# Block means of v copied by VectorE, identity matmuls ahead of the scores, masking in one operation and moved steps in an attention + two-MLP kernel

## The chip, the cores and the metric

The kernel runs on one core of one Trainium2 chip. The metric is the device time of one execution in microseconds; the median of three runs is given, and one execution was profiled. Engines are named as the profile names them: PE (TensorE, matmuls; PEld its weight loads), DVE (VectorE), ACT (ScalarE), POOL (GpSimd), SP (SyncE, which here issues most DMAs).

## The reference

The input is a batch of 2, with 8 heads, 768 positions and a head size of 64. Each query attends to its neighbours at a distance under 16 and, besides, to one summary for each block of 32 positions: the maximum of the block's keys, and the mean of its values.

```python
k_sum = k.reshape(B, H, nb, block, D).max(axis=3)
v_sum = v.reshape(B, H, nb, block, D).mean(axis=3)
scores_l = scale * np.matmul(q, k.transpose(0, 1, 3, 2))
mask_l = np.abs(pos[:, None] - pos[None, :]) < window
scores_s = scale * np.einsum('bhsd,bhnd->bhsn', q, k_sum) + np.log(block)
scores_all = np.concatenate([np.where(mask_l, scores_l, -1e9), scores_s], axis=-1)
a = np.exp(scores_all - np.max(scores_all, axis=-1, keepdims=True))
a = a / (np.sum(a, axis=-1, keepdims=True) + 1e-09)
attn = np.matmul(a, np.concatenate([v, v_sum], axis=2))
...
x = attn as 1536 tokens of 512
x = (silu(x @ w_gate) * (x @ w_val)) @ w_out      # 512 -> 1536 -> 512
out = relu(x @ w_in) ** 2 @ w_out2                # 512 -> 2048 -> 512
```

The weights arrive as 64-bit floats (read as pairs of 32-bit words), so that they have to be converted on the chip.

## The kernel before

**Tiling.** The 1536 tokens are three sets of 512. A set has four pairs of heads, and a pair has two units of 4 blocks of 64 queries. One unit is a tile of 128 rows (2 heads x 64 queries) by 480 columns: for each of the 4 blocks 96 neighbouring keys (64 and a halo of 16 on either side) and 24 summaries. Keys come in tiles `kw`, queries in `q`, values in `v`: 96 rows of values and under them, in rows 96 to 119, the 24 block means of v.

**Steps of a unit.** `sum_k` takes the blocks' maxima (DVE) and `fill_k` copies them into `kw` (POOL or DVE). `scores` or `masked_scores` multiplies (PE, into a PSUM bank). In the first set the mask is added by PE (`ident` times `mask`), and `tops` takes row maxima (DVE); in the other sets `masked` scales, masks and takes minima on DVE, four operations of 120 columns each with a read of the accumulator. Exponentials follow on ACT (`masked_exps`, `exps`), then `recip`, a normalisation (`norm` on POOL or `norm_act` on ACT), `turn` (transposes on PE), `turned` (a copy by ACT), `product` with v (PE), and `high` and `low`, which split the result into a float32r part and a rest.

**Means of v.** `load_vn` loads a tile of 4 heads' v, `sum_v` adds it up on POOL in three steps, `mean_v` multiplies by `sel` on PE, `keep_v` copies the result into `vs`, and `load_vs` spreads it by DMA into rows 96 to 119 of the `v` tiles: from ACT's queue in the prologue (eight DMAs), from SP's later.

**Weights.** A chunk of weights is converted in five pieces: `magnitude` (ACT), then clamp, shift, sign, low (DVE). `split_chunk` then makes `whi` (ACT) and `wlo` (DVE). Every product is three matmuls (xh whi, xl whi, xh wlo). Converted chunks are stored to DRAM (`keep_chunk`) and loaded again for the later sets (`load_kept`).

**Order.** It is written by hand; nothing reorders it. The prologue is the attention of set 0: a loop over t = 0 to 11 runs one step of several units in each turn. Then come 36 periods "12" (12 chunks of the first MLP for each of three sets) and 48 periods "34" (16 for each set). A period has three slots: the multiplications of w_gate (j = 0), those of w_val (j = 1), and the second product of the period before. The attention of sets 1 and 2 is placed into these slots by `place`: `first`, `after` and `late` are lists of steps for each slot, a pair of heads takes 6 slots (two periods), and `s` is its slot of scores. `pieces_of` puts the pieces of the weights into the slots.

**Pools.** There are two PSUM banks for the attention of the sets 1 and 2 (`ps_a`), two for the first products (`ps_m`) and four for the second (`ps_c`). The tile `raw` has three buffers, `wf` three, `v` three, `q` two, `kw` three, `vn` two. A DMA issue waits, besides the buffer, for the landing of the DMA that stood eight issues before it.

## Time and profile before

| | us |
|---|---|
| median of 3 runs (662.18 to 662.78) | 662.76 |
| the profiled execution | 661.7 |
| its span | 660.0 |
| PE busy | 627.9 (95%) |
| DVE busy | 417.9 (63%) |
| ACT busy | 340.0 (52%) |
| POOL busy | 40.1 (6%) |

The shares are means over the whole span. The prologue ends near 57 us, set 0 of the first MLP near 180 us, the periods "12" near 391 us. A matmul's end is modelled, so that a busy PE can still run below its peak; a gap before one is real. In a row of the timeline the bracket gives the idle time before the instruction and what ended it. The granted clock is TensorE's, 1.00 for 2.4 GHz and 0.50 for 1.2 GHz.

### The profile page before, as it was taken

The page shows a single profiled execution, that of the slowest core. Times are in us where ns is not written, and L with a number is a line of the kernel's source. Part 1 is how long each engine was busy: PE and PEld are TensorE (multiplying, and loading weights), DVE is VectorE, ACT ScalarE, POOL GpSimd, SP SyncE. Part 2 cuts the span into 40 slices and gives each one's busy share as a digit, 9 for nine tenths or more (in the row PEclk, how much of TensorE's full clock was granted, in tenths as well). Part 3 has the DMA queues.
Part 4 walks back from the last instruction along what each step waited for, and adds up shares of the span by engine and source line. Part 5 has one row for each costly group of instructions (what it writes and reads, how often), then busy time and mean ns, then how long its engine had stood idle before and what let it go on. Part 6 is the DMA issues. An engine that isn't in the chain of part 4 may idle for free.

```text
span 660.0 us, 8823 instructions
## 1 busy us (share of the span) xinstructions
PE 627.9 (95%) x3208; PEld 517.1 (78%) x3208; DVE 417.9 (63%) x622; ACT 340.0 (52%) x606; POOL 40.1 (6%) x54
## 2 busy tenths in 40 slices
PE   5768889999999999999999999999999999999997
PEld 4756678777888888788888888888888888888885
DVE  3667998998675777678776656444455444544443
ACT  1555388668457677845434435444444444444442
POOL 4423500000000000000000000000000000000000
PEclk9889999999999999999999999999999999999999
DMA  8989999862976885656858233222143222342211
GB/s 338 325 290 354 299 329 319 279 209 94 345 265 229 273 278 205 197 181 217 294 189 288 98 121 128 96 100 97 66 160 128 96 95 96 107 149 96 95 49 64
DMA packets 52908, 126.02 MB, mean 191 GB/s; under 512 B 9856, under 2 KB 16000, under 8 KB 51328
## 3 DMA queue, kind: packets, MB, share of 16 engines
q1 hardware_dynamic: 51232, 125.06, 55.7%
q10 hardware_dynamic: 1632, 0.39, 0.4%
q8 instruction: 25, 0.41, 0.3%
q14 instruction: 19, 0.16, 0.1%
HBM read 103.28 MB, written 20.97 MB: 188 GB/s over the span
## 4 chain that ended last, share of the span: by engine, by line
PE 78%; DVE 9%; ACT 5%; DMA 5%; issue 2%; POOL 1%; SPq 0%; DVEq 0%; ACTq 0%; POOLq 0%
PE bank L501 22%; PE bank L510 20%; PE bank L529 19%; PE bank L527 11%; DMA kept<-wf 2%; DVE wlo L211 2%; PE bank L445 1%; DVE wf L179 1%; DMA v<-vs 1%; ACT s L403 1%; DVE wf L174 1%; ACT wf L160 1%; PE bank L348 1%; DVE wf L163 1%; PE bank L433 1%
## 5 line engine op out<-in xcount | busy, mean ns | idle before, releaser
L211 DVE TENSOR_TENSOR wlo<-wf,whi 128x1024 fp32r<-128x1024 f32 (+2 forms) x85 | 123.5, 1454 | 52.5 <-ACT whi L210 51.6
L210 ACT CAST whi<-wf 128x1024 fp32r<-128x1024 f32 (+2 forms) x85 | 104.1, 1225 | 90.5 <-PE bank L529 50.0
L501 PE MATMUL bank<-xh,whi 128*128 128x512 f32 x288 | 116.5, 405 | 3.8 <-ACT g L729 1.9
L501 PE MATMUL bank<-xh,wlo 128*128 128x512 f32 x288 | 113.2, 393 | 4.5 <-DVE wlo L211 4.5
L501 PE MATMUL bank<-xl,whi 128*128 128x512 f32 x288 | 112.7, 391 | 0.0
L746 DVE TENSOR_TENSOR r<-r 128x512 f32<-128x512 f32 x48 | 33.2, 692 | 86.4 <-ACT hh L745 86.4
L529 PE MATMUL bank<-whi,hl 128*128 128x512 f32 x192 | 74.8, 390 | 0.0
L529 PE MATMUL bank<-whi,hh 128*128 128x512 f32 x192 | 74.7, 389 | 0.0
L529 PE MATMUL bank<-wlo,hh 128*128 128x512 f32 x192 | 74.7, 389 | 0.0
L510 PE MATMUL bank<-xh,whi 128*128 128x512 f32 x192 | 74.7, 389 | 0.0
L510 PE MATMUL bank<-xl,whi 128*128 128x512 f32 x192 | 74.7, 389 | 0.0
L510 PE MATMUL bank<-xh,wlo 128*128 128x512 f32 x192 | 74.7, 389 | 0.0
L744 ACT ACTIVATE r<-bank 128x512 f32<-128x512 f32 x48 | 28.7, 598 | 86.6 <-PE bank L510 86.6
L501 PEld LDWEIGHTS bank<-xh,wlo 128*128 128x128 f32 x288 | 54.2, 188 | 18.0 <-DVE wlo L211 6.6
L501 PEld LDWEIGHTS bank<-xh,whi 128*128 128x128 f32 x288 | 54.2, 188 | 16.5 <-ACT g L729 2.9
L734 ACT CAST hh<-g 128x512 fp32r<-128x512 f32 x36 | 22.2, 618 | 81.1 <-DVE g L733 81.1
L501 PEld LDWEIGHTS bank<-xl,whi 128*128 128x128 f32 x288 | 54.3, 189 | 10.1
L527 PE MATMUL bank<-hh,whi 128*128 128x512 f32 x144 | 57.5, 400 | 0.0
L527 PE MATMUL bank<-hl,whi 128*128 128x512 f32 x144 | 56.2, 390 | 0.0
L527 PE MATMUL bank<-hh,wlo 128*128 128x512 f32 x144 | 56.2, 390 | 0.0
L174 DVE SCALAR_TENSOR_TENSOR wf<-raw,wf 128x1024 uint32<-128x1024 uint32 (+2 forms) x29 | 41.9, 1446 | 0.3
L529 PEld LDWEIGHTS bank<-whi,hh 128*128 128x128 f32 x192 | 36.1, 188 | 7.6
(73 smaller groups left out, 907.0 us busy)
## 6 DMA issues: line engine op xcount, KB each, us to landing
wf<-kept SPq DMA_DIRECT2D x120, 256.0 KB
raw<-in_w_dram SPq DMA_DIRECT2D x44, 512.0 KB
kept<-wf SPq DMA_DIRECT2D x28, 512.0 KB
raw<-in_w_dram SPq DMA_DIRECT2D x12, 1024.0 KB
wf<-kept SPq DMA_DIRECT2D x24, 512.0 KB
kw<-in_kW_dram SPq DMA_DIRECT2D x8, 768.0 KB
q<-in_qB_dram SPq DMA_DIRECT2D x8, 512.0 KB
vn<-in_vN_dram SPq DMA_DIRECT2D x4, 768.0 KB
```

What stands on the lines that cost most here:

```text
L160: nc.scalar.activation(f32(w), f32(hw), ACTF.Abs)
L163: nc.vector.tensor_scalar(out=f32(w), in0=f32(w), scalar1=HI_MIN, scalar2=HI_MAX, op0=ALU.max, op1=ALU.min)
L174: nc.vector.scalar_tensor_tensor(out=w, in0=hw, scalar=0xC0000000, in1=w, op0=ALU.bitwise_and, op1=ALU.bitwise_or)
L210: lambda: nc.scalar.copy(hi[:, cs], t),
L211: lambda: nc.vector.tensor_sub(lo[:, cs], t, f32(hi[:, cs])),
L501: nc.tensor.matmul(p, w[a][:, c], x[i][kk], start=(kk == 0 and n == 0), stop=(kk == KD - 1 and n == 2),)
L510: nc.tensor.matmul(p, w[a][:, c], x[i][kk], start=(kk == 0 and n == 0), stop=(kk == KD - 1 and n == 2),)
L527: nc.tensor.matmul(ps[t], w[a][:, c], h[e], start=(f == 0 and n == 0), stop=(f == last and n == 2))
L529: nc.tensor.matmul(ps[t], h[e][:, t * P:(t + 1) * P], w[a][:, off:off + DM], start=(f == 0 and n == 0), stop=(f == last and n == 2),)
L734: nc.scalar.copy(h[0], g)
L744: nc.scalar.activation(r, p, ACTF.Relu)
L746: nc.vector.tensor_mul(r, r, r)
```

## The change

- `mean_v` writes its four heads at rows 0, 32, 64 and 96 (`sel` and `vs` have 128 rows), so that DVE can copy the means into rows 96 to 119 of `v`: in the prologue `put_vs` issues two copies for each pair of heads in place of DMAs on ACT's queue. In the later sets SP's DMAs stay. `mean_v` moves from turn 0 to turn 1, behind `recip` and `norm`.
- Eight matmuls of the identity with itself stand ahead of the first scores.
- `masked` becomes one scaled addition over 480 columns with `maskn` (made by POOL in turn 8) and one minimum.
- `product` of both units writes one bank; `high_both` and `low_both` take it in one operation each, one slot after the second product.
- In `place`, scores and masking move one slot earlier. In `pieces_of`, `keep_chunk` and `load_kept` move from slot 2 to slot 1, and `magnitude` to just behind the first copy of h.
- The first additions of the upper heads' `sum_v` move one turn earlier, the load of the first `v` behind the second pair's loads.

```diff
-    def sum_v(b, g, engine):
+    def sum_v(b, g, steps=(4, 2, 1)):
...
+        for n in steps:
+            nc.gpsimd.tensor_add(t[:, :, 0:n, :], t[:, :, 0:n, :], t[:, :, n:2 * n, :])
...
-                ps[0:4 * NS, 0:D], sel[:, i, :], t[:, i, 0, :], start=(i == 0), stop=(i == VG - 1)
+                ps[:, 0:D], sel[:, i, :, :], t[:, i, 0, :], start=(i == 0), stop=(i == VG - 1)
...
-        def load_vs(self, queue):
+        def put_vs(self, put):
...
-                    r = (h % 4) * NS
-                    queue.dma_start(
-                        out=self.v[WIN:W, at:at + n, j * D:(j + 1) * D],
-                        in_=vs[r:r + NS, b, h // 4, :].unsqueeze(1).to_broadcast([NS, n, D]),
+                    r = 32 * (h % 4)
+                    put(
+                        self.v[WIN:W, at:at + n, j * D:(j + 1) * D],
+                        vs[r:r + NS, b, h // 4, :].unsqueeze(1).to_broadcast([NS, n, D]),
...
-            for i in range(UB):
-                mv = self.variant(j, i)
-                c = slice(i * W, (i + 1) * W)
-                nc.vector.tensor_tensor_reduce(
-                    out=s[:, c], in0=ps[:, c], in1=mask[:, mv, :],
-                    scale=-SCALE, scalar=3.0e38, op0=ALU.add, op1=ALU.min,
-                    accum_out=m[:, i:i + 1],
-                )
+            nc.vector.scalar_tensor_tensor(
+                out=sv, in0=ps[:, 0:UB * W].rearrange("p (n c) -> p n c", c=W), scalar=-SCALE,
+                in1=maskn[:, mv:mv + UB, :], op0=ALU.mult, op1=ALU.add,
+            )
+            nc.vector.tensor_reduce(out=m, in_=sv, op=ALU.min, axis=AX.X)
...
+        def high_both(self, copy):
+            copy(self.x[0][self.hp], self.st["po", 0])
+
+        def low_both(self):
+            nc.vector.tensor_sub(self.x[1][self.hp], self.st.pop(("po", 0)), f32(self.x[0][self.hp]))
...
+        for hp, p in enumerate(pairs):
+            for j in range(2):
+                at(after, d0 + 6 * hp + 3 + j, lambda p=p, j=j: p.scores(j))
...
-                at(after, s + j, lambda p=p, j=j: p.scores(j))
-                at(first, s + j + 1, lambda p=p, j=j: p.masked(j))
+                at(first, s + j, lambda p=p, j=j: p.masked(j))
...
-                at(after, s + 10 + j, lambda p=p, j=j: p.product(j, ps_a))
-                at(first, s + 11 + j, lambda p=p, j=j: p.high(j, nc.vector.tensor_copy))
-                at(first, s + 11 + j, lambda p=p, j=j: p.low(j))
+                at(after, s + 10 + j, lambda p=p, j=j: p.product(j, ps_a, True))
+            at(first, s + 12, lambda p=p: p.high_both(nc.vector.tensor_copy))
+            at(first, s + 12, p.low_both)
...
+        busy = bank(ps_m)
+        for i in range(WARM):
+            nc.tensor.matmul(busy[:, 0:P], ident, ident, start=True, stop=True)
...
-            if t in (0, 5):
+            if t in (1, 5):
                 mean_v(0, t // 5, ps_m)
                 keep_v(0, t // 5)
-            go("recip", t - 1)
-            go("norm", t - 1)
+                pairs[t // 5 * 2].put_vs(nc.vector.tensor_copy)
+            elif t in (2, 6):
+                pairs[t // 6 * 2 + 1].put_vs(nc.vector.tensor_copy)
...
-            if t in (0, 5):
-                pairs[t // 5 * 2].load_vs(nc.scalar)
-                pairs[t // 5 * 2 + 1].load_vs(nc.scalar)
...
                     if s == 1:
                         load_words(k + 4)
-                    if s == 2:
                         keep_chunk(k + 1)
                         load_kept(k + 3)
-                        cv[k + 3] = convert_chunk(k + 3)
-                        cv[k + 3][0]()
...
                         nc.scalar.copy(h[0], g)
+                        magnitude()
                         c2[3]()
```

In the prologue, on DVE, from the maxima of the first pair's keys (`ks`, line 332, 334 in the changed kernel) on, it stands before:

```order
L332 TENSOR_REDUCE ks_192<-kw 128x24
L340 COPY kw<-ks_192 128x4x24 x2
L367 TENSOR_REDUCE m<-bank 128x4
L370 TENSOR_SCALAR m<-m 128x4
L276 COPY vs<-bank 96x64
L332 TENSOR_REDUCE ks_234<-kw 128x24
L367 TENSOR_REDUCE m<-bank 128x4
L370 TENSOR_SCALAR m<-m 128x4
```

and after the change:

```order
L334 TENSOR_REDUCE ks_202<-kw 128x24
L342 COPY kw<-ks_202 128x4x24 x2
L369 TENSOR_REDUCE m<-bank 128x4
L372 TENSOR_SCALAR m<-m 128x4
L334 TENSOR_REDUCE ks_239<-kw 128x24
L369 TENSOR_REDUCE m<-bank 128x4
L372 TENSOR_SCALAR m<-m 128x4
L413 TENSOR_SCALAR r<-r 128x4
L414 RECIPROCAL r<-r 128x4
L278 COPY vs<-bank 128x64
L324 COPY v<-vs 24x8x64 x2
```

The copy of the means (`vs`) has moved behind the second pair's maxima and the next unit's row maxima (`m`), and two copies into `v` follow it.

In the periods, on ACT, one pair of heads' exponentials (`s,rr`, 403 or 406) stand before among the steps of the weights (`wf` by `magnitude`, 160 or 164; `whi`), with `hh` the copy of h and `a` the copy of the transposes:

```order
L437 COPY a<-bank 120x512
L734 CAST hh<-g 128x512
L437 COPY a<-bank 120x512
L403 ACT_TABLE_LOAD
L403 ACTIVATE s,rr<-s,m 128x120 x8
L160 ACTIVATE wf<-raw 128x1536
L210 CAST whi<-wf 128x1536
```

and after the change:

```order
L440 COPY a<-bank 120x512
L762 CAST hh<-g 128x512
L164 ACTIVATE wf<-raw 128x1536
L440 COPY a<-bank 120x512
L406 ACT_TABLE_LOAD
L406 ACTIVATE s,rr<-s,m 128x120 x8
L214 CAST whi<-wf 128x1536
```

`magnitude` has moved from behind the exponentials to just behind `hh`.

In the periods, on DVE, the masking of a unit (390, or 393 and 397) stands before so, among clamp and shift (163, 168), `wlo` (211), the product `g` (733), sign (174), `hl` (736) and low (179):

```order
L168 TENSOR_SCALAR wf<-wf 128x1536
L211 TENSOR_TENSOR wlo<-wf,whi 128x1536
L733 TENSOR_TENSOR g<-g,bank 128x512
L174 SCALAR_TENSOR_TENSOR wf<-raw,wf 128x1536
L736 TENSOR_TENSOR hl<-g,hh 128x512
L390 ISA s,m<-bank,mask 128x120
L390 ISA m 128x1
...
L179 SCALAR_TENSOR_TENSOR wf<-raw,wf 128x1536
L390 ISA s,m<-bank,mask 128x120
L390 ISA m 128x1
```

and after the change, in a pair that also has the former pair's `xh` and `xl` (468, 471) in the shared bank:

```order
L167 TENSOR_SCALAR wf<-wf 128x1536
L172 TENSOR_SCALAR wf<-wf 128x1536
L468 CAST xh_611<-bank 128x512
L471 TENSOR_TENSOR xl_615<-bank,xh_611 128x512
L418 TENSOR_SCALAR rr<-rr 128x8
L419 RECIPROCAL rr<-rr 128x8
L393 SCALAR_TENSOR_TENSOR s<-bank,maskn 128x480
L397 TENSOR_REDUCE m<-s 128x4
L215 TENSOR_TENSOR wlo<-wf,whi 128x1536
L761 TENSOR_TENSOR g<-g,bank 128x512
L178 SCALAR_TENSOR_TENSOR wf<-raw,wf 128x1536
L765 TENSOR_TENSOR hl<-g,hh 128x512
```

The first unit's masking has moved from behind `hl` to ahead of `wlo`, and the copy and the subtraction of the shared bank stand ahead of it.

## Rows read from the trace of the kernel before

**Rows 1.** The page: engine, busy us (share of the span), xinstructions.

```profile
PE 627.9 (95%) x3208; PEld 517.1 (78%) x3208; DVE 417.9 (63%) x622; ACT 340.0 (52%) x606; POOL 40.1 (6%) x54
```

**Rows 2.** Stretches: us, then busy us (xinstructions), granted clock, DMA share, GB/s.

```profile
core 0: us, PE busy (x) PEld busy (x) DVE busy (x) ACT busy (x) POOL busy (x), PEclk, DMA share, GB/s
...
6.70:12.20 5.50, 5.49 (x26) 5.50 (x27) 1.14 (x2) 0.45 (x1) 3.29 (x3) 1.00 1.03 375
12.20:26.00 13.80, 8.50 (x72) 7.87 (x71) 7.63 (x18) 8.63 (x36) 4.25 (x8) 1.00 1.03 346
26.00:29.20 3.20, 3.02 (x24) 2.91 (x25) 3.10 (x7) 0.85 (x4) 0.14 (x1) 0.50 1.06 326
44.70:48.50 3.80, 3.75 (x25) 2.92 (x27) 3.37 (x6) 1.03 (x4) 0.99 (x1) 0.50 0.74 224
97.00:119.00 22.00, 20.87 (x130) 16.88 (x129) 20.33 (x38) 17.03 (x36) 1.58 (x2) 1.00 0.97 312
180.00:391.00 211.00, 211.00 (x1079) 174.00 (x1078) 147.48 (x232) 117.68 (x207) 1.90 (x6) 1.00 0.64 220
```

**Rows 3.** Timeline of the prologue: start us, us, engine line op [idle before, releaser].

```profile
8.75 3.56 POOL L263 TENSOR_TENSOR vn<-vn 128x768 f32<-128x768 f32 x3 [3.87 <-DMA vn<-in_vN_dram]
...
13.71 0.22 DVE L276 COPY vs<-bank 96x64 f32<-96x64 f32 x1 [2.04 <-PE bank L271]
...
15.17 0.48 PE L357 MATMUL bank<-kw,q 128*128 128x120 f32 x2 [1.50 <-POOL kw L340]
...
26.18 1.12 PE L445 MATMUL bank<-a,v 120*64 120x64 f32 x14 [2.17 <-DMA v<-vs]
...
35.05 3.48 ACTq L322 DMA_DIRECT2D v<-vs  x4
...
44.75 1.27 PE L445 MATMUL bank<-a,v 120*64 120x64 f32 x16 [2.28 <-DMA v<-vs]
...
52.41 0.69 PE L445 MATMUL bank<-a,v 120*64 120x64 f32 x16
```

**Rows 4.** Line 322, issues by ACT: duration ns min/median/max, first and last start us.

```profile
L322 ACTq DMA_DIRECT2D v<-vs x8: 790/795/1397, 14.0 to 37.7; - x8
```

**Rows 5.** Timeline where the prologue meets the periods.

```profile
55.15 6.28 POOL L263 TENSOR_TENSOR vn<-vn 128x768 f32<-128x768 f32 x3 [7.88 <-DMA vn<-in_vN_dram]
...
61.37 0.26 POOL L340 COPY kw<-ks 128x96 f32<-128x96 f32 x1
...
64.48 1.04 PE L348 MATMUL bank<-kw,q 128*128 128x120 f32 x8
```

**Rows 6.** Timeline of the periods: waits of PE and DVE.

```profile
71.58 0.50 PE L501 MATMUL bank<-xh,wlo 128*128 128x512 f32 x1 [1.95 <-DVE wlo L211]
...
96.78 0.62 PE L433 MATMUL bank<-ident,s 128*120 128x128 f32 x4 [1.18 <-DVE m L390]
...
110.34 0.96 DVE L163 TENSOR_SCALAR wf<-wf 128x1536 f32<-128x1536 f32 x1 [1.50 <-ACT wf L160]
...
118.85 0.62 PE L433 MATMUL bank<-ident,s 128*120 128x128 f32 x4 [1.13 <-DVE m L390]
...
159.21 0.50 PE L501 MATMUL bank<-xh,wlo 128*128 128x512 f32 x1 [0.70 <-DVE wlo L211]
```

**Rows 7.** Groups by form: line engine op xcount | busy us, mean ns | idle before.

```profile
L733 DVE TENSOR_TENSOR g<-g,bank 128x512 f32<-128x512 f32 x36 | 24.6, 685 | 23.7 <-PE bank L501 22.9 <-PE bank L433 0.6 <-ACT g L729 0.2
L390 DVE CUSTOM_DVE_ANT_0 s<-bank,mask 128x120 f32<-128x120 f32 x64 | 14.1, 277 | 0.4 <-PE bank L348 0.4
L163 DVE TENSOR_SCALAR wf<-wf 128x1024 f32<-128x1024 f32 x17 | 11.7, 687 | 1.7 <-ACT wf L160 1.7
L452 DVE CAST xh<-bank 128x256 fp32r<-128x256 f32 x16 | 6.7, 421 | 11.3 <-PE bank L445 11.3
L367 DVE TENSOR_REDUCE m<-bank 128x4 f32<-128x480 f32 x8 | 5.2, 652 | 5.9 <-PE bank L358 5.9
```

**Rows 8.** Timeline of the later stage: the copy from the products' bank, the next scores.

```profile
248.37 0.42 DVE L452 CAST xh<-bank 128x256 fp32r<-128x256 f32 x1 [2.00 <-PE bank L445]
...
251.10 1.04 PE L348 MATMUL bank<-kw,q 128*128 128x120 f32 x8
```

More of the change, by code (lines that the diff above doesn't have):

```diff
@@ L256, in load_vn @@
         nc.sync.dma_start(out=t, in_=vN[b, g].rearrange("r m -> (r m)").rearrange("(p m) -> p m", p=P))
-    def sum_v(b, g, engine):
+    def sum_v(b, g, steps=(4, 2, 1)):
         t = vn_t[b, g].rearrange("p (s c d) -> p s c d", s=VG, d=D)
-        n = VT // VG // 2
-        while n:
-            engine.tensor_add(t[:, :, 0:n, :], t[:, :, 0:n, :], t[:, :, n:2 * n, :])
-            n //= 2
+        for n in steps:
+            nc.gpsimd.tensor_add(t[:, :, 0:n, :], t[:, :, 0:n, :], t[:, :, n:2 * n, :])
     def mean_v(b, g, pool):
@@ L437, in turned, with product @@
             nc.scalar.copy(a, self.st.pop(("pt", j))[0:W, :])
-        def product(self, j, pool):
-            ps = self.st["po", j] = bank(pool)
+        def product(self, j, pool, shared=False):
+            if shared and j:
+                ps = self.st["po", 0]
+            else:
+                ps = self.st["po", j] = bank(pool)
             a = self.st.pop(("a", j))
+            at = j * UT if shared else 0
             for i in range(UB):
@@ L476, in place @@
             at(first, s - 3, p.load_v)
-            at(first, s + 7, lambda p=p: p.load_vs(nc.sync))
+            at(first, s + 7, lambda p=p: p.put_vs(nc.sync.dma_start))
             for j in range(2):
-                at(after, s + j, lambda p=p, j=j: p.scores(j))
-                at(first, s + j + 1, lambda p=p, j=j: p.masked(j))
+                at(first, s + j, lambda p=p, j=j: p.masked(j))
                 at(late, s + 3, lambda p=p, j=j: p.exps(j))
@@ L559, in block_summary_attention__gated_mlp__relu2_mlp @@
         load_vn(0, 0)
-        pairs[0].load_v()
         pairs[1].load_k()
         pairs[1].load_q()
+        pairs[0].load_v()
         load_words(0)
@@ L586, in block_summary_attention__gated_mlp__relu2_mlp @@
             nc.gpsimd.affine_select(
-                out=sel, in_=sel, compare_op=ALU.is_ge, fill=0.0,
-                base=base, pattern=[[sign, VG], [-(VG + 1) * sign, 4 * NS]], channel_multiplier=VG * sign,
-            )
+                out=sel, in_=sel, compare_op=ALU.is_ge, fill=0.0, base=base,
+                pattern=[[sign, VG], [-32 * VG * sign, 4], [-(VG + 1) * sign, 32]], channel_multiplier=VG * sign,
+            )
+        busy = bank(ps_m)
+        for i in range(WARM):
+            nc.tensor.matmul(busy[:, 0:P], ident, ident, start=True, stop=True)
         pairs[0].sum_k()
@@ L631, in block_summary_attention__gated_mlp__relu2_mlp @@
                 pairs[t // 2 + 1].fill_k(nc.gpsimd)
-            if t == 4:
-                sum_v(0, 1, nc.gpsimd)
+            if t == 3:
+                sum_v(0, 1, (4,))
+            elif t == 4:
+                sum_v(0, 1, (2, 1))
             go("product", t - 3, ps_c)
@@ L659, in block_summary_attention__gated_mlp__relu2_mlp @@
                 tick()
+                for c, mv in ((slice(0, 1), 0), (slice(1, 5), 1), (slice(5, 6), 2)):
+                    n = c.stop - c.start
+                    nc.gpsimd.tensor_scalar_mul(
+                        maskn[:, c, :], mask[:, mv:mv + 1, :].to_broadcast([P, n, W]), -SCALE
+                    )
             elif t == 9:
@@ L677, in block_summary_attention__gated_mlp__relu2_mlp @@
             at(first, 0, lambda g=g: load_vn(1, g))
-            at(late, 1 + 2 * g, lambda g=g: sum_v(1, g, nc.gpsimd))
+            at(late, 1 + 2 * g, lambda g=g: sum_v(1, g))
             at(after, 7 + g, lambda g=g: mean_v(1, g, ps_a))
@@ L715, in block_summary_attention__gated_mlp__relu2_mlp, with magnitude @@
             h = None
+            def magnitude():
+                cv[k + 3] = convert_chunk(k + 3)
+                cv[k + 3][0]()
             if kind == "12":
@@ L742, in block_summary_attention__gated_mlp__relu2_mlp @@
                 pieces_of(0, 1)
+                magnitude()
                 r = t_p.tile([P, TS], F32, tag="t", name="r")
```

21 lines of the change are left out of this document (14 added, 7 removed).

## The prediction

> **What bounds the kernel now.** I read the page first: TensorE (PE) is busy 95% of the 660.0 us span [rows 1]. That is an average over two parts. In the table of stretches PE is busy without a gap from 180 to 391 us, and PE and VectorE (DVE) are both busy for most of 97 to 119 us, 20.87 and 20.33 of 22 us [rows 2]. The last wait of PE for another engine in the periods ends at 159.21 us [rows 6]; behind it the number of matmuls sets the time, and this change takes none away. So everything that can move lies before 159 us, in the prologue (to about 57 us, the attention of the first set of tokens) and in the periods behind it, in which DVE still converts the weights.
>
> In the prologue the timeline shows what PE waits for [rows 3]. It idles 1.50 us before 15.17 us, because the maxima of the second pair's k stood behind the copy of the v means (13.71 us, itself waiting 2.04 us for PE). ACT issues, four at a time, the eight DMAs that spread the v means into the v tiles, at about 0.8 us each and 1.4 for the longest [rows 4]: some 3.8 us from 14.0 on, 3.48 us from 35.05 on. PE then waits 2.17 us (26.18) and 2.28 us (44.75) for those DMAs to land. From 6.7 to 12.2 us 26 matmuls take 5.49 us, 0.21 each, against 0.12 in the next stretch, though both read a granted clock of 1.00; at 26.0 to 29.2 and 44.7 to 48.5 us it reads 0.50 [rows 2].
>
> In the periods the waits repeat every two periods (one pair of heads): PE stands 1.18 us at 96.78 and 1.13 us at 118.85, 22.07 us apart, for DVE's masking (line 390), and DVE stands 1.50 us at 110.34 for ACT's `magnitude` (line 160), which is queued behind eight exponentials [rows 6]. The first is a bank that the masking frees late; the second is an order on ACT. Between PE's wait at 71.58 and its last at 159.21 lie 87.6 us, 4.0 such pairs of periods.
>
> **Prologue.** (1) The maxima of the second pair no longer wait for the copy of the v means. They need their load, and the fill on GpSimd (POOL) comes behind its sum of v, which runs from 8.75 to 12.31 us [rows 3]; the fill can end near 12.8 and the scores that started at 15.17 can start near 12.9: 2.3 us. (2) The eight DMA issues leave ACT: 3.8 and 3.5 us. (3) The two waits for their landing go: 2.17 and 2.28 us. (4) DVE gets eight copies of 24 x 512 elements. No row shows one: by the rate of the 128x1024 scalar operation (687 ns, so 0.34 for half of it) they cost 2.7 us together, by that of the 512-element product from PSUM (685 ns) 5.5 us [rows 7]. They are float32 from SBUF to SBUF with one input, as in the first row, so I take 0.4 each, 3.2 us. DVE is busy 7.63 of 13.8 us there [rows 2], but the copies stand in front of the next unit's row maxima, so I count half, 1.6 us, on the path. (5) The sum of v for the upper heads, 3.56 us if it is as long as the first, is cut in two around a normalisation and no longer stands whole ahead of it: no figure of its own. (6) Eight matmuls of the identity run while the first loads come. At the pace of the first scores (0.42 us for the two passes of one) they take 3.4 us, on an engine whose first work begins at 6.7 us: no cost. If the clock is then granted, the first scores shorten by up to 2.7 us; but the loads in (1) cap what follows from that, and that cap is already counted.
>
> Added up: 2.3 + 3.5 (of the two issue blocks I count the second; the first overlaps 1) + 2.17 + 2.28 - 1.6 = 8.7 us. These waits are not wholly in series: around the one at 26.18 DVE converts the first chunk in any case. I take 7.5 us. Low bound 3 us (1 and a part of 2; conversions and loads hold the rest), high bound 12 us (all in full, and half of the 3.02 and 3.75 us of slow PE work besides).
>
> For the copies of (4) there is a rule that speaks against the change. The rows: POOL's sum of v took 6.28 us at 55.15, where DVE works beside it, and 3.56 us at 8.75 [rows 3, 5]. The Trainium skill, SBUF — State Buffer, section "Who interferes with whom", says that DVE and GpSimd share one port pair, and that a float32 copy in a two-port mode takes it for the whole instruction. By that rule each copy could hold POOL's normalisations up, and the gain would be smaller by up to the copies' own 3.2 us; the sum above leaves this out.
>
> **From prologue to periods.** The scores of the second set move one slot earlier, in front of PE's second product of period 1. They need the fill of kw, which POOL does after its sum of v: the sum 55.15 to 61.43, the fill at 61.37, the scores at 64.48 [rows 5]. With PE 7.5 us earlier and one slot sooner, it would come to them near 51, while the loads (SP's queue no longer waits for the spreading DMAs to land) bring the fill to perhaps 55. So PE will wait there, 3 to 5 us. I cost it at nothing, since DVE's conversions of chunks 2 and 3 run on meanwhile and set when period 2 starts; if that cover is gone, it costs up to 5 us of the 7.5.
>
> **Periods.** (7) Masking in one operation: line 390 keeps DVE busy 14.1 us in 16 units, 0.88 per unit; in its place come a product of 480 columns from PSUM (685 ns for 512, so 0.64) and a minimum (652 ns), 1.29 per unit, +0.82 us on DVE per pair. (8) Both units' products in one bank: four operations of 256 columns (0.42 us each) become a copy and a subtraction of 512 (0.68 each): -0.32 us [rows 7]. DVE's 20.33 us become 20.8. (9) `magnitude` moves ahead of the exponentials on ACT: the 1.50 us wait goes. What is late next is the exponentials, by the length of one `magnitude`, with 5 us of ACT's 22 idle (17.03 busy) to take it [rows 2]. (10) Masking one slot earlier frees the bank before `turn` wants it: PE's 1.13 to 1.18 us go. The pair of periods is then a little above both DVE's 20.8 and PE's 20.87, near 21.1 instead of 22.07: 1.0 us, 4.0 times, 4 us. Bounds: 1.2 (0.3 each, if the two engines wait for each other) to 6. (11) SP stores the converted chunk and loads the kept one a slot earlier, ahead of its four small DMAs; `magnitude` is the first to read behind it, and if a load is late there, the wait of (9) comes back: that is the low bound.
>
> **A new wait, priced.** In one bank, the next scores can't begin until the subtraction has freed it. In the later stage DVE is at that copy at 248.37, having waited 2.00 us, and PE reaches the scores at 251.10 [rows 8]: 0.68 + 0.68 us end at 249.7, 1.4 us in time. From 159 us to the end I count no change.
>
> **Sum.** The profiled execution took 661.7 us, 1.7 around its span. 661.7 - 7.5 - 4.0 = 650.2. It stands 1.06 below the median of the three, 662.76, so the forecast for the median is **651.2 us**.
>
> **Rivals.** *A smaller gain (20%).* PE falls to the half clock between small groups, or POOL and the loads set the pace; prologue 3, periods 2: 662.8 - 5 = 658. For it: the three slow stretches [rows 2], and a PE that idles from about 5 to 6.7 us after its identity matmuls. The Trainium skill, TensorE: Matmul & The Clock Gate, says under "What's actually happening" that the throttled state is the default and activity releases it; the slow start here agrees, and by that rule the identity matmuls favour the high end. *A larger gain (13%).* All of 12 in the prologue and 5 in the periods: 646. *The moved scores stop PE (7%, slower).* v for the means lands no sooner than now, because the loads and not the spreading DMAs set that date; PE stands at the moved scores until the fill at 61.6, and the second product of period 1, which now ends before 64.48, comes behind it, about 0.9 us late [rows 5]; the prologue's gain is gone, and if DVE's 1.50 is only replaced by another wait, (7) and (8) add 0.5 a pair: 662.8 + 0.9 + 2.0 = 665.7. It decides once the fill ends after about 58 us. *It does not do what it says (5%, no change):* the copies wait for the means as long as the DMAs did.
>
> **How the numbers follow.** My forecast, 648 to 655, has 55%; the rivals 20, 13, 7 and 5%. The range holds the smaller gain to 659 and the larger to 645. A measurement of this kernel tells about 0.2%, 1.3 us, from no change. Faster: 55 + 20 + 13 = 88%; same 5%; slower 7%.
>
> **What would show it.** Right: no issues of v by ACT in the prologue; PE's last product of the prologue near 44 instead of 52.41 [rows 3]; no DVE wait for line 160 ahead of the clamp; PE's waits for the masking gone and pairs of periods near 21 us; the stage behind 159 as long as before. Wrong: PE standing at the moved scores with DVE idle beside it; PE waiting for the shared bank's subtraction in every pair; a granted clock of 0.50 over most of the prologue.

## The result and the profile after

The changed kernel takes 655.61 us (median of 4 runs, 654.93 to 657.85) against 662.47 us of the kernel before beside it (4 runs, 660.90 to 662.78): a ratio of 0.9907, with a 95% interval of 0.9878 to 0.9936. A second set of six runs (`changed_again` below) gave 656.65 us and 0.9898 (0.9868 to 0.9927). It is faster by about 7 us. The ten times of the changed kernel lie in two groups, six from 654.93 to 655.77 us and four from 657.61 to 657.94, and both of its profiles are of the first. The forecast was 651.2 us, range 645 to 659: the sign is right and the time lies in the range, 4.4 us above the forecast. So four tenths of the expected gain are missing, and the question is where.

The profiled execution took 654.93 us, its span is 653.2 us against 660.0. On the page PE and DVE (columns as in [rows 1]) are both busier in a shorter span:

```profile
PE 630.8 (97%) x3224; PEld 521.0 (80%) x3224; DVE 428.3 (66%) x518; ACT 340.1 (52%) x606; POOL 50.4 (8%) x57
```

Where the gain lies is read from the start of PE's first matmul in the periods 1, 4 and 10 (timeline: start us, us, engine line op [idle before, releaser]). Before:

```profile
56.86 0.50 PE L501 MATMUL bank<-xh,whi 128*128 128x512 f32 x1 [0.82 <-ACT g L729]
92.36 0.50 PE L501 MATMUL bank<-xh,whi 128*128 128x512 f32 x1 [0.66 <-ACT g L729]
157.78 0.50 PE L501 MATMUL bank<-xh,whi 128*128 128x512 f32 x1 [0.44 <-ACT g L729]
```

After:

```profile
53.49 0.50 PE L516 MATMUL bank<-xh,whi 128*128 128x512 f32 x1 [0.72 <-ACT g L757]
88.97 0.39 PE L516 MATMUL bank<-xh,whi 128*128 128x512 f32 x1
151.94 0.50 PE L516 MATMUL bank<-xh,whi 128*128 128x512 f32 x1 [0.48 <-ACT g L757]
```

At period 1 the changed kernel is 3.37 us ahead, at period 4 3.39, at period 10 5.84, at the end 6.8. Of the last 0.9 us, 0.70 are the wait at 159.21 [rows 6], which is gone. So the prologue gave 3.4 us where 7.5 were forecast, and the periods 3.4 where 4.0 were forecast. The long stage behind is as it was: 982 matmuls in 191.00 us, in both without a gap.

The stretches show what took the place of the waits that went (columns as in [rows 2]). Before, from the first scores to period 1, and the periods:

```profile
6.70:56.86 50.16, 38.82 (x325) 33.88 (x325) 28.33 (x55) 26.55 (x88) 17.97 (x21) 0.90 0.98 335
58.30:157.00 98.70, 90.19 (x515) 72.36 (x514) 91.11 (x152) 68.43 (x138) 14.86 (x14) 1.00 0.84 281
```

After:

```profile
6.70:53.49 46.79, 36.73 (x324) 31.86 (x324) 35.54 (x63) 26.41 (x88) 24.02 (x24) 0.93 1.03 356
57.00:149.00 92.00, 87.76 (x498) 71.79 (x499) 90.77 (x99) 66.48 (x136) 13.63 (x12) 0.98 0.86 286
...
192.40:383.40 191.00, 191.00 (x982) 157.43 (x981) 134.51 (x156) 107.97 (x195) 4.31 (x4) 1.00 0.63 213
```

In the prologue PE idles 10.1 us in place of 11.3: nearly all of the waits are still there. The other 2.1 us of the 3.37 are PE's own: the same work keeps it busy 36.7 us in place of 38.8, at a mean granted clock of 0.93 in place of 0.90. DVE is busy 35.5 us in place of 28.3, POOL 24.0 in place of 18.0 (5.2 of it the filling of `maskn`), ACT as long as before. In the periods DVE is busy 90.8 of 92 us, where before it had 7.6 us to spare: it has become the bound.

Whom PE waits for has changed. PE's groups from 12 to 57 us (busy us, mean ns | idle just before, by releaser), before:

```profile
L357 PE MATMUL bank<-kw,q 128*128 128x120 f32 x52 | 10.8, 293 | 3.3 <-ACT s L378 1.8 <-POOL kw L340 1.5
L445 PE MATMUL bank<-a,v 120*64 120x64 f32 x128 | 7.3, 262 | 4.4 <-DMA v<-vs 4.4
L433 PE MATMUL bank<-ident,s 128*120 128x128 f32 x32 | 6.1, 324 | 1.1 <-POOL s L421 1.1
```

and after:

```profile
L359 PE MATMUL bank<-kw,q 128*128 128x120 f32 x48 | 9.9, 289 | 3.4 <-ACT s L380 2.5 <-POOL kw L342 0.9
L452 PE MATMUL bank<-a,v 120*64 120x64 f32 x128 | 6.4, 251 | 0.0
L436 PE MATMUL bank<-ident,s 128*120 128x128 f32 x32 | 5.8, 310 | 4.3 <-POOL s L424 4.3
```

The 4.4 us of waits for the spread means are gone, as forecast; 4.3 us of waits for POOL's normalisation stand there now, in place of 1.1. The timeline of the changed prologue shows why POOL is late:

```profile
14.41 0.45 PE L359 MATMUL bank<-kw,q 128*128 128x120 f32 x2 [2.47 <-ACT s L380]
17.34 0.85 DVE L324 COPY v<-vs 24x512 f32<-24x512 f32 x2
19.41 1.55 DVE L324 COPY v<-vs 24x512 f32<-24x512 f32 x2
19.52 1.15 POOL L424 TENSOR_TENSOR s<-s,r 128x480 f32<-128x480 f32 x1 [3.66 <-DVE r L414]
...
25.33 2.79 POOL L266 TENSOR_TENSOR vn<-vn 128x768 f32<-128x768 f32 x1
26.48 2.72 DVE L183 SCALAR_TENSOR_TENSOR wf<-raw,wf 128x1024 uint32<-128x1024 uint32 x1
30.40 0.99 POOL L424 TENSOR_TENSOR s<-s,r 128x480 f32<-128x480 f32 x1 [2.29 <-DVE r L414]
31.44 0.65 PE L436 MATMUL bank<-ident,s 128*120 128x128 f32 x4 [1.96 <-POOL s L424]
```

POOL's normalisation waits for the reciprocals that DVE forms, and these stand in DVE's queue behind the copies and behind the conversion of the first chunk, one of whose operations (line 183) takes 2.72 us while POOL adds up v; it ends at 29.20 us, 1.08 after POOL's addition (28.12). So PE waits 1.96 us at 31.44 for POOL, which waited 2.29 us for DVE.

### The profile page after: what moved, and what is told of

It reads as the page before. It is cut to its first block, busy times and chain, and to the rows that moved or that the text cites. A ratio compares the mean times of both kernels' runs of the same rounds, so it can differ in the third digit from the quotient of the medians.

```text
span 653.2 us, 8749 instructions
## 1 busy us (share of the span) xinstructions
PE 630.8 (97%) x3224; PEld 521.0 (80%) x3224; DVE 428.3 (66%) x518; ACT 340.1 (52%) x606; POOL 50.4 (8%) x57
## 4 chain that ended last, share of the span: by engine, by line
PE 82%; DVE 7%; DMA 5%; ACT 3%; issue 2%; POOL 0%; SPq 0%; DVEq 0%; POOLq 0%; ACTq 0%
PE bank L516 25%; PE bank L525 20%; PE bank L544 20%; PE bank L542 12%; DMA raw<-in_w_dram 2%; DMA kw<-in_kW_dram 2%; PE bank L350 2%; PE bank L452 1%; DMA q<-in_qB_dram 1%; DVE wf L183 1%; DVE wf L178 1%; PE bank L436 1%; ACT wf L164 1%; DVE wlo L215 1%; DVE wf L167 1%
## 5 line engine op out<-in xcount | busy, mean ns | idle before, releaser
L762 ACT CAST hh<-g 128x512 fp32r<-128x512 f32 x36 | 22.2, 617 | 81.6 <-DVE g L761 81.6
L542 PE MATMUL bank<-hh,wlo 128*128 128x512 f32 x144 | 56.5, 392 | 0.0
L178 DVE SCALAR_TENSOR_TENSOR wf<-raw,wf 128x1024 uint32<-128x1024 uint32 (+2 forms) x29 | 42.4, 1462 | 0.3
L183 DVE SCALAR_TENSOR_TENSOR wf<-raw,wf 128x1024 uint32<-128x1024 uint32 (+2 forms) x29 | 42.3, 1458 | 0.2
```

Of the source, the lines that this page charges most:

```text
L178: nc.vector.scalar_tensor_tensor(out=w, in0=hw, scalar=0xC0000000, in1=w, op0=ALU.bitwise_and, op1=ALU.bitwise_or)
L183: nc.vector.scalar_tensor_tensor(out=w, in0=lw, scalar=29, in1=w, op0=ALU.logical_shift_right, op1=ALU.bitwise_or)
L542: nc.tensor.matmul(ps[t], w[a][:, c], h[e], start=(f == 0 and n == 0), stop=(f == last and n == 2))
L762: nc.scalar.copy(h[0], g)
```

## Experiments

Each run changes one thing in the changed kernel unless it says otherwise. Three groups ran, each on a chip of its own beside the kernel before; ratios are to the kernel before of the same group. The last two columns are read from each run's one trace: the start of period 1, and the time from there to the start of period 10. The second leaves out the prologue, but not wholly: it moves with how much of POOL's first sum still runs beside period 1. DVE's operation on line 172 takes 1.65 us beside it at 55.95 in the changed kernel, 0.96 behind it at 58.90 in no_warm, and runs that differ from the changed kernel only ahead of period 1 need 97.70 to 98.72 us.

| run | median us (range, runs) | ratio to before (95%) | period 1 at | to period 10 |
|---|---|---|---|---|
| before | | 1 | 56.86 | 100.92 |
| changed kernel | 655.61 (654.93 to 657.85, 4) | 0.9907 (0.9878 to 0.9936) | 53.49 | 98.45 |
| changed_again | 656.65 (654.95 to 657.94, 6) | 0.9898 (0.9868 to 0.9927) | 54.23 | 98.55 |
| spread_by_dma | 661.48 (659.21 to 664.39, 12) | 0.9975 (0.9955 to 0.9995) | 60.18 | 98.56 |
| copies_by_act | 657.04 (655.92 to 658.64, 6) | 0.9909 (0.9879 to 0.9939) | 55.85 | 97.70 |
| sum_v_whole | 655.39 (655.25 to 657.14, 6) | 0.9886 (0.9860 to 0.9913) | 53.72 | 98.72 |
| no_warm | 656.82 (655.86 to 657.48, 6) | 0.9900 (0.9874 to 0.9926) | 56.44 | 97.78 |
| early_fill | 659.00 (657.44 to 660.00, 6) | 0.9931 (0.9906 to 0.9956) | 54.00 | 100.49 |
| magnitude_late | 664.81 (663.97 to 666.99, 12) | 1.0026 (1.0008 to 1.0044) | 54.14 | 104.60 |
| scores_late | 660.35 (659.64 to 662.56, 12) | 0.9961 (0.9945 to 0.9977) | 56.41 | 102.43 |
| banks_apart | 658.35 (657.72 to 659.14, 6) | 0.9925 (0.9907 to 0.9944) | 56.44 | 99.92 |
| old_masking | 654.98 (653.36 to 655.38, 5) | 0.9867 (0.9838 to 0.9896) | 56.37 | 95.92 |
| mask_ks | 655.30 (655.03 to 655.50, 4) | 0.9879 (0.9857 to 0.9900) | 56.21 | 96.11 |
| mask_ks_banks | 656.25 (654.37 to 659.07, 6) | 0.9899 (0.9875 to 0.9923) | 56.42 | 96.87 |

The theory they started from: DVE's queue alone sets the time from 17 to 149 us, and the missing gain went into the copies. The rival: PE, or the loads, set it, and the gain went into PE's waits at the moved scores.

**The copies.** First back to the DMAs:

```diff
-                pairs[t // 5 * 2].put_vs(nc.vector.tensor_copy)
-            elif t in (2, 6):
-                pairs[t // 6 * 2 + 1].put_vs(nc.vector.tensor_copy)
...
             go("turned", t - 2)
+            if t in (1, 5):
+                pairs[t // 5 * 2].put_vs(nc.scalar.dma_start)
+                pairs[t // 5 * 2 + 1].put_vs(nc.scalar.dma_start)
```

> The changed kernel with the v means spread by eight DMAs on ScalarE's queue (at the end of turns 1 and 5), as in the kernel before, in place of VectorE's copies. By the prediction's sum the copies are worth 3.5 + 2.17 + 2.28 - 1.6 = 6.35 us: 662 us, as slow as before. Theory now (where the copies end, another engine is next, so that most of the removed waits lay beside other work): 1 to 3 us, 656.6 to 658.6 us. Rival (the copies cost what they save): 655.6 us.

It is 4.8 us slower than the changed kernel of its group, all of it in the prologue (period 1 at 60.18, the periods unchanged). That is nearer to the prediction's 6.35 than to the theory's 1 to 3. PE stands at the products, 1.24 us at 27.83 and longer at the second set's (timeline of PE):

```profile
48.41 0.45 PE L452 MATMUL bank<-a,v 120*64 120x64 f32 x2 [4.58 <-DMA v<-vs]
```

Then the same copies on ACT, behind each turn's exponentials:

```diff
-                pairs[t // 5 * 2].put_vs(nc.vector.tensor_copy)
-            elif t in (2, 6):
-                pairs[t // 6 * 2 + 1].put_vs(nc.vector.tensor_copy)
...
             go("turned", t - 2)
+            if t in (1, 5):
+                pairs[t // 5 * 2].put_vs(nc.scalar.copy)
+            elif t in (2, 6):
+                pairs[t // 6 * 2 + 1].put_vs(nc.scalar.copy)
```

> The eight copies of the v means by ScalarE (behind each turn's exponentials) in place of VectorE. Theory (VectorE's queue sets the time from 17 to 149 us): 3.2 us of copies stand in the chain of waits of the changed kernel (0.84 + 0.85 + 1.54), and go from it; ScalarE takes 8 x 0.6 = 4.8 us, of which it has idle 3.5 and 3.4 us in these turns: 652 to 654.5 us. Rival (loads or TensorE pace the prologue, VectorE only fills it): 655.6 us as the changed kernel, or up to 1.5 us more if the copies delay the exponentials.

Nothing changes that can be measured, though 4.8 us of copies left DVE. The theory that DVE alone bounds the prologue falls here: ACT became late at once, and DVE (timeline) now waits for it:

```profile
37.23 0.42 DVE L463 TENSOR_TENSOR xl<-bank,xh 128x256 fp32r<-128x256 f32 x1 [1.31 <-ACT xh L459]
42.23 0.42 DVE L463 TENSOR_TENSOR xl<-bank,xh 128x256 fp32r<-128x256 f32 x1 [2.38 <-ACT xh L459]
```

In the prologue DVE, ACT, POOL and PE hand each unit on in turn, and each has little to spare; what is taken from one is soon waited for at the next.

**The sum of v.** The split of step (5) undone:

```diff
-            if t == 3:
-                sum_v(0, 1, (4,))
-            elif t == 4:
-                sum_v(0, 1, (2, 1))
+            if t == 4:
+                sum_v(0, 1)
```

> The upper heads' sum of v whole, one turn later, as in the kernel before. Theory (the first addition on GpSimd, 25.33 to 28.12 us, held VectorE's operation at 26.48 for 2.72 us in place of 1.23): 1.5 us come back on VectorE, while the whole sum of 3.56 us then stands ahead of a normalisation that began at 33.38 us and delays it by up to 1.9 us: 654.1 to 656.0 us, and the operation on line 183 at 1.2 us. Rival (the long operation there is due to loads, not GpSimd): it stays at 2.7 us and the time rises by 1.9 us to 657.5 us.

The long operation goes, as the theory said, but POOL's sum now meets a tiny one on DVE, which grows from 0.17 to 1.57 us (timeline of DVE):

```profile
26.46 1.22 DVE L183 SCALAR_TENSOR_TENSOR wf<-raw,wf 128x1024 uint32<-128x1024 uint32 x1
28.29 0.17 DVE L372 TENSOR_SCALAR m<-m 128x4 f32<-128x4 f32 x1
30.51 1.57 DVE L372 TENSOR_SCALAR m<-m 128x4 f32<-128x4 f32 x1
```

The time does not move. That POOL's addition, not a load, made line 183 slow is shown; that the split costs or gains anything is not.

**The identity matmuls.** `WARM = 0` in place of 8:

> The changed kernel without its eight identity matmuls. Theory (VectorE's queue sets the time from 17 to 149 us): they only bring the first row maxima from 10.49 us (before) to 10.18 us, so this run is 0.3 us slower than the changed kernel: 655.9 us. Rival (the clock after them matters, and stretches at 0.50 return): 16 slow matmuls cost up to 2.7 us: 658.3 us.

No difference beyond the noise: 0.9900 against 0.9898 of the changed kernel. Its period 1 starts at 56.44, but so it does in runs that keep these matmuls; the next experiment tells why.

**The same kernel again.**

> The changed kernel once more, unaltered, beside the other three of this group. What it tells: how far its time moves by the place of the stretches at a granted clock of 0.50, of which its first profile has three before 70 us (near 22.7, 40.8 and 64.5 us) and those of two of its variants two, at other places. Theory: 655.6 us with single runs 1.5 us to either side, and the start of period 1 anywhere from 53.5 to 56.5 us. Rival (the stretches are fixed by the order of the work): a start of period 1 within 0.3 us of 53.49, and runs within 0.5 us.

Six profiles of this study have the same code up to 50 us: the two of the changed kernel, early_fill and magnitude_late begin period 1 at 53.49 to 54.23, scores_late and banks_apart at 56.41 and 56.44. What differs is where PE's granted clock is at 0.50 (1.2 GHz). Two stretches tell it, one from the end of PE's wait near 31.45 to DVE's copy of the means, one from the end of PE's last wait for POOL's normalisation to period 1. In scores_late:

```profile
31.46:35.96 4.50, 4.50 (x29) 4.43 (x30) 1.56 (x5) 3.75 (x14) 2.85 (x5) 0.67 1.02 320
47.69:56.41 8.72, 7.91 (x54) 5.85 (x54) 6.17 (x6) 4.64 (x7) 8.64 (x5) 0.80 0.92 288
```

in the changed kernel, with one ahead of the first wait:

```profile
22.50:26.10 3.60, 3.60 (x32) 3.33 (x32) 3.50 (x7) 1.96 (x9) 2.53 (x3) 0.62 1.03 391
31.44:34.53 3.09, 3.09 (x28) 3.02 (x30) 1.56 (x4) 2.50 (x13) 2.85 (x5) 1.00 1.09 289
46.27:53.49 7.22, 6.50 (x54) 4.72 (x54) 6.07 (x6) 4.62 (x7) 5.93 (x4) 1.00 1.05 358
```

and in changed_again:

```profile
30.55:35.27 4.72, 4.72 (x29) 4.65 (x31) 1.56 (x5) 3.75 (x14) 2.85 (x5) 0.64 1.04 323
```

Both reach the transposes near 31.45 us (31.44 and 31.46), since both wait there for POOL. In the changed kernel's profile the slow stretch lay ahead of that wait and was covered by it; in scores_late PE idled 2.97 us in place of 1.96, was then at 0.50, and the means of v came 1.4 us later (35.13 against 33.71). The first stretch is 1.41 us longer in scores_late, the second 1.50; together they are the 2.9 us by which it begins period 1 later. changed_again, magnitude_late and early_fill lose about as much in one of the two alone (4.72 and 4.68 us in the first, 8.75 in the second), and their second pair's scores began 0.9 to 1.0 us earlier (13.39 to 13.52 us against 14.41); banks_apart loses in the first, and is 1.3 us late ahead of it (at 0.50 from 12.7 to 19.3 us). So of the prologue's gain 3 us depend on where these stretches fall; the 53.49 of the profile above was the good case. What makes them fall here or there in one code is open. The kernel before was profiled once, so that it is not known how far its own 56.86 moves.

**The seam.** The maxima and both fills of the second set's first keys a slot earlier, ahead of POOL's sum:

```diff
-            at(late, s - 2, p.sum_k)
-            at(late, s - 2, lambda p=p: p.fill_k(nc.gpsimd))
+            e = 3 if i == 1 and hp == 0 else 2
+            at(late, s - e, p.sum_k)
+            at(late, s - e, lambda p=p: p.fill_k(nc.gpsimd))
```

> The changed kernel with the maxima of the second set's first keys and both fills one slot earlier, so that GpSimd does the fills ahead of its sum of v and VectorE the maxima ahead of its operation on line 183. TensorE's two waits at the moved scores (1.78 and 1.81 us in the changed kernel) should go. Theory (VectorE, not TensorE, sets the time from 55 to 149 us): the waits go and the time stays, 654.8 to 655.8 us; TensorE then waits elsewhere before 150 us, for VectorE. Rival (TensorE's waits at the moved scores are where the prologue's gain went): 652 us.

In the changed kernel PE stands twice at the moved scores, first for a fill behind POOL's sum, then for a fill whose maxima stand behind DVE's line 183 (timeline):

```profile
46.18 5.18 POOL L684 TENSOR_SCALAR maskn<-mask 128x120 f32<-128x120 f32 x3
52.66 5.39 POOL L266 TENSOR_TENSOR vn<-vn 128x768 f32<-128x768 f32 x3 [1.29 <-DMA vn<-in_vN_dram]
57.99 0.26 POOL L342 COPY kw<-ks 128x96 f32<-128x96 f32 x1
58.31 1.15 PE L350 MATMUL bank<-kw,q 128*128 128x120 f32 x8 [1.78 <-POOL kw L342]
62.06 0.94 DVE L334 TENSOR_REDUCE ks<-kw 128x24 f32<-128x768 f32 x1
63.06 0.93 POOL L342 COPY kw<-ks 128x96 f32<-128x96 f32 x1 [4.81 <-DVE ks L334]
64.05 1.21 PE L350 MATMUL bank<-kw,q 128*128 128x120 f32 x5 [1.81 <-POOL kw L342]
```

With the fills first, the wait at the first of them is gone, one of 1.91 stays at the second, a new one of 2.15 for DVE comes, and the median is 2.3 us higher, though the intervals of the ratios overlap. PE's waits were exchanged, not removed, so this run alone does not rule the rival out. What speaks against it is that in the changed kernel DVE, from 54.96 to 91.48 us, never idles more than 0.1 us: PE's waits here lie beside a DVE that is late in any case. DVE's operations grew, because POOL's two sums now run on end beside them (timeline of this run):

```profile
62.90 11.71 POOL L266 TENSOR_TENSOR vn<-vn 128x768 f32<-128x768 f32 x6
63.77 2.48 DVE L172 TENSOR_SCALAR wf<-wf 128x1536 uint32<-128x1536 uint32 x1
69.47 0.53 PE L517 MATMUL bank<-xh,wlo 128*128 128x512 f32 x1 [2.15 <-DVE wlo L215]
69.94 2.80 DVE L178 SCALAR_TENSOR_TENSOR wf<-raw,wf 128x1536 uint32<-128x1536 uint32 x1
```

These two take 0.96 and 1.75 us undisturbed (rows at 63.90 and 58.12 us of the changed kernel). From the first to the third clamp (line 167) DVE needs 21.54 us here (55.45 to 76.99), 19.54 in the changed kernel (54.96 to 74.50): 2.0 us, nearly the whole difference. Here, up to period 4, it is DVE that counts.

**The order in the periods.** `magnitude` back behind the exponentials:

```diff
                     if s == 1:
                         load_words(k + 4)
                         keep_chunk(k + 1)
                         load_kept(k + 3)
+                    if s == 2:
+                        magnitude()
...
                         nc.scalar.copy(h[0], g)
-                        magnitude()
```

> The changed kernel with magnitude behind the exponentials again, a slot later. Theory (VectorE sets the periods, busy without a break from 55 to 149 us): its waits of 1.55, 1.50, 1.51 and 2.35 us come back, 5 to 7 us in all: 661 to 662.5 us. Rival (both engines share the bound, and TensorE has its own 20.9 us per pair): the waits come back but cost half: 658 to 659 us.

8.2 us slower than the changed kernel, and slower than before. DVE's waits come back longer than they were before (1.55, 2.31, 2.32 and 3.13 us), and they hold up the shared bank, at which PE's scores now stand (timeline):

```profile
108.28 0.96 DVE L167 TENSOR_SCALAR wf<-wf 128x1536 f32<-128x1536 f32 x1 [2.31 <-ACT wf L164]
110.86 0.69 DVE L471 TENSOR_TENSOR xl<-bank,xh 128x512 fp32r<-128x512 f32 x1
111.81 2.03 PE L350 MATMUL bank<-kw,q 128*128 128x120 f32 x8 [3.59 <-DVE rr L418]
```

The row names the DVE instruction that started just ahead; the scores begin 0.3 us after the subtraction of the bank ends. Behind this wait PE's granted clock is at 0.50 (stretch):

```profile
111.80:117.00 5.20, 5.19 (x16) 4.50 (x17) 5.17 (x7) 4.02 (x10) 0.00 (x0) 0.50 0.93 308
```

The pair from period 4 to 6 takes 28.41 us, 6.2 more than in the changed kernel; 3.8 of them are PE's longer waits (3.59 here, 1.05 at 91.24, against 0.81), the other 2.4 the slower pace behind them. So the early `magnitude` is what makes the shared bank and the early scores bearable: the parts are not worth their own sum.

Scores and masking back in their old slots:

```diff
-                at(after, d0 + 6 * hp + 3 + j, lambda p=p, j=j: p.scores(j))
...
+                at(after, s + j, lambda p=p, j=j: p.scores(j))
-                at(first, s + j, lambda p=p, j=j: p.masked(j))
+                at(first, s + j + 1, lambda p=p, j=j: p.masked(j))
```

> The changed kernel with scores and masking of the later sets in their old slots, one slot later. By the prediction's step (10), TensorE's waits of 1.13 to 1.18 us per pair come back: 4 us, 660 us. Theory now (VectorE's work sets the time from 55 to 149 us, and TensorE's waits lie beside it): those waits come back, the two at the moved scores (1.8 and 1.8 to 2.4 us) go, and the time moves by less than 1.5 us: 655 to 657.5 us. Rival (TensorE's waits at the moved scores are where the prologue's gain went): 652 to 653 us.

The theory of a DVE that covers everything falls a second time: the ratio is 0.0063 higher, 4.2 us, and the periods alone are 3.9 us longer (4.7 against no_warm, which starts period 1 as late). PE's waits are back (timeline of PE; a third like them, of 1.04 us, stands at 140.79):

```profile
96.36 0.62 PE L436 MATMUL bank<-ident,s 128*120 128x128 f32 x4 [1.17 <-DVE s L393]
118.57 0.62 PE L436 MATMUL bank<-ident,s 128*120 128x128 f32 x4 [1.03 <-DVE s L393]
```

The prediction had 1.13 to 1.18 us a pair for them in step (10), in a sum of 4 us for the periods.

Separate banks for the products:

```diff
-                at(after, s + 10 + j, lambda p=p, j=j: p.product(j, ps_a, True))
-            at(first, s + 12, lambda p=p: p.high_both(nc.vector.tensor_copy))
-            at(first, s + 12, p.low_both)
+                at(after, s + 10 + j, lambda p=p, j=j: p.product(j, ps_a))
+                at(first, s + 11 + j, lambda p=p, j=j: p.high(j, nc.vector.tensor_copy))
+                at(first, s + 11 + j, lambda p=p, j=j: p.low(j))
```

> The changed kernel with both units' products in banks of their own again, each copied and subtracted in its slot. By the prediction's step (8), VectorE gets 0.32 us per pair more: +1.3 us, 657 to 658 us, if VectorE sets the periods. Rival (the wait of TensorE's scores for the shared bank, 0.81 us near 108, is what counts): that wait goes, and the time falls by up to 0.8 us, to 655 us.

0.0027 slower in the ratio, 1.8 us, and 1.4 in the periods, against 1.3 forecast; the intervals of the ratios overlap. And it doesn't lie where the forecast put it. The pair from period 4 to 6 is 2.4 us longer (24.57 against 22.2), with a wait of PE for a bank here too (timeline of DVE and PE):

```profile
107.44 0.42 DVE L463 TENSOR_TENSOR xl<-bank,xh 128x256 fp32r<-128x256 f32 x1
107.97 1.00 PE L452 MATMUL bank<-a,v 120*64 120x64 f32 x16 [1.81 <-issue]
```

The bracket names no releaser, but the attention has two banks, the next pair's early scores took the second, and the product starts 0.1 us after DVE has subtracted what was in the first. In mask_ks_banks PE waits 1.79 us in the same place, and again until 0.1 us after the subtraction. From 108.0 to 111.6 us the granted clock is 0.53. The next two pairs are shorter than in the changed kernel (20.77 and 18.96 against 21.2 and 19.6). So this run exchanges the shared bank's wait of 0.8 us near 108 for a longer one, and what the shared bank alone costs was not measured.

**The masking.** The four fused operations of before in the new slots, without `maskn`:

```diff
-            nc.vector.scalar_tensor_tensor(
...
-            nc.vector.tensor_reduce(out=m, in_=sv, op=ALU.min, axis=AX.X)
+            for i in range(UB):
+                mv = self.variant(j, i)
+                c = slice(i * W, (i + 1) * W)
+                nc.vector.tensor_tensor_reduce(
+                    out=s[:, c], in0=ps[:, c], in1=mask[:, mv, :],
+                    scale=-SCALE, scalar=3.0e38, op0=ALU.add, op1=ALU.min,
+                    accum_out=m[:, i:i + 1],
+                )
```

> Masking by four fused operations per unit as before, 0.81 us from start to start in place of 1.25; the slots as in the changed kernel; the three GpSimd operations that fill maskn are gone. Theory (VectorE sets the periods): 8 x 0.44 = 3.5 us leave VectorE, but TensorE idles only 1.6 us between 64 and 152 us, so 654.0 to 654.6 us. Rival (TensorE's order of work sets them): 655.6 us. A third way (the fused operation brings back a wait for the masking): 657 us.

The periods shorten by 2.6 us (95.92 against 98.5), by 1.8 against runs that start period 1 as late as this one (no_warm 97.78, copies_by_act 97.70), and the pair from period 6 to 8 to 20.77, in which PE has no gap. By the whole time it is 1 to 2 us, and the intervals of the ratios overlap. By the traces the one masking operation is a part of the change that costs, some 0.4 us of DVE per unit. But banks_apart, which keeps it, has that pair at 20.77 too: with the new masking alone or the shared bank alone PE has no gap there, with both it has. The edit also takes the filling of `maskn` off POOL; from period 4 to 10, far behind it, 1.2 us are gained (61.76 against 62.97).

Two mixtures with this masking tried to take out PE's remaining waits: in mask_ks the maxima (`sum_k`) of the second set's first keys come one slot earlier, not the fills; mask_ks_banks has separate banks besides.

> The changed kernel with the four fused masking operations of before, and the maxima of the second set's first keys (not the fills) one slot earlier on VectorE, ahead of its operation on line 183. Fused masking alone gave 654.98 us. There TensorE waited 2.78 us at the second moved scores for a fill that needs these maxima. Theory (with 3.5 us of masking gone from VectorE, TensorE's waits begin to count): the 2.78 us go, and 1 to 2 us of them from the time: 653 to 654 us. Rival (VectorE is still the later one there): 655 us.

> As the one with fused masking and early maxima, and the products in banks of their own besides. With fused masking VectorE has 0.8 us per pair to spare, so that the 0.32 us per pair of the separate copies cost nothing and TensorE's wait for the shared bank (0.81 us near 108) goes: 0 to 0.8 us less than that kernel. Rival (VectorE is still the bound): 1.3 us more.

Neither is faster than old_masking, and none of the three is told apart from the changed kernel by the whole time. In mask_ks PE's wait at the second moved scores falls from 2.78 to 1.91 us and a wait of 1.47 for `wlo` comes behind it.

## Why the prediction was right, and where it failed

**What bounds the kernel** held: everything that moved lies before 159 us, and the stage behind is unchanged.

**The prologue (7.5 us) is the step that failed.** Measured: 2.6 to 3.4 us in four profiles, 0.4 in two, by where the slow stretches of PE's clock fall; and of the 3.4 only 1.3 are waits that went (in changed_again 2.4 of 2.6; there PE is slower ahead of its waits, at 38.6 us busy). PE's last product of the prologue starts at 49.05, not near 44. By terms:
- (1) 2.3 us: the fill ended at 12.84 as forecast (12.8), but the scores started at 14.41, only 0.8 us ahead of 15.17 [rows 3] (13.39 to 14.43 in the other five profiles of this code). Next late was the bank: ACT's first exponentials, behind a table load of 1.28 us at 11.53, had to free it.
- (2) and (3) less (4), 6.35 us in all: the waits for the DMAs went entirely. Going back to DMAs in this order costs 4.8. But the 3.5 us of (2) are time of ACT; near the second block of issues PE waited, besides the 2.28 of (3), only 1.13 us, at 41.53 for DVE's `wlo`, and a wait like it, 1.62 us at 40.37, is still there. The copies took 4.8 us in place of 3.2 (0.42 each, but the second pair's 1.55 for two where POOL normalises beside them).
- (5) and (6), no figure and no cost: undoing either moves the time by nothing that can be measured.

The error was to add these up with a discount of 1.2 us. Every wait that went was followed by another engine that was nearly as late: 4.4 us for the DMAs became 4.3 us for POOL, behind reciprocals in DVE's longer queue. The question that would have shown it: of 50 us PE idles 11.3, DVE gets 7.2 us more work (the copies, and what POOL's work beside it costs), and all four engines must still hand over in turn; whose result comes next?

**The skill's rule on the port** (The Trainium skill, SBUF — State Buffer, "Who interferes with whom": whoever issues first holds the pair that DVE and GpSimd share for the whole instruction, and the other blocks) was left out of the sum, with up to 3.2 us at stake. The trace agrees with it, but the loser was mostly DVE: its copies lost 0.7 us per second pair and POOL's product beside them 0.15, and its line 183, begun 1.15 us after POOL's addition, lost 1.5 to it. It should have stood in the sum with the sign it has there.

**The seam** was costed at nothing, and that held (DVE is without a gap there), though its numbers did not: PE came to the moved scores at 56.5 and not 51, the fill ended at 58.25 (61.63 before [rows 5]) and not 55, and a second wait of 1.81 us stood behind the first. The run that took the first away was slower, since POOL's sums then ran on beside DVE. The rival of the moved scores that stop PE named 58 us as the point from which it decides; the fill ended just there, and the wait cost 1.78 us that DVE covered.

**The periods (4 us) held**: 3.4 measured, none of it before period 4, where POOL's sums still run beside DVE, and 0.16, 0.95, 1.35 and 0.94 in the four pairs from there. The shared bank's operations are 0.68 and 0.69 us, as forecast, and the masking is 1.28 per unit, forecast 1.29 (groups by form, 90 to 134 us):

```profile
L397 DVE TENSOR_REDUCE m<-s 128x4 f32<-128x480 f32 x4 | 2.6, 653 | 0.1
L393 DVE SCALAR_TENSOR_TENSOR s<-bank,maskn 128x480 f32<-128x480 f32 x4 | 2.5, 629 | 0.0
```

DVE's waits for `magnitude` between 89 and 155 us are gone (one of 1.63 at the start of period 1 stays), and PE's for the masking too; the pair from period 6 to 8 takes 21.15 us, forecast 21.1, the one from 4 to 6 22.2. Step (9) was mis-sized in what it carries: undone alone it costs 8.2 us, not 6 (four times 1.5), because it also keeps the shared bank in time, and PE is at 0.50 behind the waits that come when it does not. And "in time" was right for the later stage and 0.8 us late in the period near 108 us: one of the signs named as wrong, at a size that did not decide.

**The rivals.** The smaller gain (658, of prologue 3 and periods 2) got the prologue, the forecast got the periods; the result stands between them, 2.4 us from one and 4.4 from the other. Its reasons were the right ones: the half clock, and POOL setting the pace. The forecast's own 648 to 655 us, with 55%, was missed by 0.6 us (1.7 in the second set); the time lies in the whole range because that also holds the smaller gain. And that period 1 starts 3.4 us earlier in the profile is in part luck of the clock.

## What to carry to other kernels

Where four engines hand a unit on in turn, a removed wait is worth what the next engine in the ring leaves of it: list the idle time of the engine that should be the bound by releaser, add the new work to each other engine's queue, and see whose result is then last. Work moved to DVE or POOL is priced with what runs on the other at that moment. And one part of a change can carry another (here the early `magnitude` the shared bank), so that undoing parts one by one gives more than the whole.

## What the runs showed of the hardware

- DVE's instructions grow while POOL adds in SBUF: a scalar operation on 128x1536 from 0.96 to 2.48 us, one with two inputs on 128x1024 from 1.22 to 2.72, one of four columns from 0.17 to 1.57. POOL's three additions take 3.56 us where DVE does little and 5.4 to 7.2 us beside its conversions, and three small operations that fill `maskn` took 5.18.
- The same code has PE's stretches at 0.50 in different places from one execution to the next. One ahead of PE's wait near 31.45 cost nothing; one behind it cost 1.4 to 1.6 us, and one behind the last wait for POOL 1.5. A wait of PE can thus cost more than its length: behind one of 3.59 us in magnitude_late PE lost 2.4 us more at 0.50. Eight identity matmuls ahead of the first scores, with 1.5 to 1.95 us of idle between, changed nothing that could be measured.
